# W2 in four loads, nine long throwaway matmuls, the first two tiles normed in three parts, and another written-out order, in a one-core kernel of LayerNorm, a spectral filter and an MLP

## The chip, the cores and the metric

The kernel runs on one core of one Trainium2 chip. The metric is the device time of one execution in microseconds, the lower the better. The core has five engines that work side by side, each through its own list of instructions in the order given: PE (TensorE, matrix products), DVE (VectorE), ACT (ScalarE), POOL (GpSimd) and SP (SyncE, which here only issues transfers). PE reads SBUF, the on-chip memory of 128 partitions, and writes PSUM, 8 banks of 2 KB per partition; DVE and ACT bring results from PSUM back to SBUF. Engines wait for each other through semaphores; a transfer (DMA) has a semaphore of its own.

## What is computed

The input x has 2048 tokens of 640 numbers in bf16. Cut to what matters:

```python
xn = layernorm(x, axis=-1)                       # 2048 x 640
X  = rfft2(xn.astype(float32), axes=(-2, -1))    # over tokens and over the 640
A  = irfft2(X * (w_r + 1j * w_i), s=(2048, 640), axes=(-2, -1)).astype(bfloat16)
h  = gelu(xn @ w1 + b1)                          # 2048 x 1536, tanh form
B  = h @ w2 + b2                                 # 2048 x 640
return x + A + B
```

The weights w1 are 640 x 1536, w2 1536 x 640, and w_r and w_i 2048 x 321.

## The kernel before

**Tiles and stages.** The tokens are cut into 16 tiles c of 128; partition p of tile c holds token 16p + c. All stages of all tiles are unrolled into about 1,100 small steps, each with a name and an engine.

- *Norm.* `x{c}` loads a tile or two (`load_x`, L455). On DVE `st{c}.0` and `st{c}.1` take the statistics of its two halves and `ag{c}` joins them. For the first two tiles `sq` (square root on ACT) and `rs` (reciprocal on DVE) give the inverse deviation, for the others `ve` on DVE and a power `rs` on POOL. `nm{c}` (DVE, L554) writes the normed tile xn. For tile 0 it has two parts, `nm0` (columns 0 to 383) and `nm0.3` (384 to 639); tile 1 has one.
- *Transposes of xn.* For tiles 0 to 3 PE transposes blocks of 128 columns against the identity (`tp`, L568) and ACT or DVE copies the result from PSUM to xnT (`tc`): in two parts for tile 0, in one for the others. Tiles 4 to 15 are transposed by DMA (`td{c}`, L560), issued on SP.
- *MLP, first product* (`h`, through the helper L411). BLOCKS makes seven groups of tiles: 0, 1, (2, 3), (4, 5), (6, 7), (8 to 11), (12 to 15). For tiles 0 and 1, `h{t}.{q}.{j}` are three matmuls of 128 columns: quarter q of the 1536 outputs, block j of the 640 inputs. From h2 on, `h{b}.{f}.0` has three matmuls and `h{b}.{f}.3` two, of 256 columns (h2 to h4) or 512 (h5, h6). `ge` on ACT is the gelu with the bias column b1col, which comes from PE step `b1mm` and ACT copy `b1cp`. A table load on ACT (`table1`, L530) stands ahead of the gelus.
- *MLP, second product.* `k{c}.{o}.{f}` and `l{c}.{o}.{f}` are three matmuls each over gT and W2, in column cuts o (CUTS: 0 to 383, 384 to 639). Ten tiles (KEEP) run early as `k`, and DVE adds x to them at once (`kk`); the others run late as `l` into the same bank as the last step of the spectral branch.
- *Spectral branch.* Folding sums on DVE (`f1`, `f2`), a product along tokens (`G{c}`, copies `gx`), one along the 640 (`b{g}`, copies `xb`), one of 32 x 32 blocks (`c{P}.{r}`, 32 small matmuls, copies `y`), the filter on DVE (`m`, `z`), the way back (`d{P}.{v}`, 32 small matmuls, copies `u`), a transpose by DMA (`vt0` to `vt15`, L706), the way back along the 640 (`e{g}`, copies `yo`), unfolding sums (`y2`, `yf`), and the last product `fin`, one matmul per piece. GROUPS gives b and e steps of three or two tiles. Each `e` step reads all 16 `vt` results. For the groups in NEAR a copy `xr{g}` (DVE or ACT) first brings a part of them next to each other.
- *End.* `os{c}.{o}` (DVE, L811) adds x or the kept sum to fin's bank, and `out` (SP, L818) stores. Tile 15 goes in three pieces (PIECES): 320, 160 and 160 columns, each with its own store; all other tiles have one store.

**Order.** Nothing chooses at run time. The string ORDER lists every step as engine:name; each engine runs its steps in that order, and SLOTS gives each buffer its place (PSUM banks among them). `Plan.place` works out from it what each step must wait for, `Plan.sync` drops waits that others imply, `Plan.emit` writes the programs. So an engine's later step waits behind its earlier one, and on SP every load, transpose and store waits behind the one before it.

**Loads.** All go through SP in ORDER's order, except b1 (ACT). The first ones are x0, x1, half of W1 by rows (`w1_00` to `w1_02`), x2 (which is tiles 2 and 3), `w1_03`, `w1_04`, the other half `w1_10` to `w1_14`. W2 comes in two halves of 960 KB, `w2_0` (of the 12 blocks of 1536 inputs the first six) and `w2_1`.

**Throwaway work.** `idle` (L444) puts matmuls of zeros into a bank that nothing reads: `idle0` 38 at the start and `idle1` 4 between the transposes of tile 0 and of tile 1.

```python
WARM = (38, 4)
...
            pe(name, lambda: [(psb(b.slot, [[1, 128]]), warm, warm, True, True) for _ in range(n)], reads=[B_warm], writes=[b], **kw)
```

Of the kernel before, what the change touches and what calls it, by code (L numbers as in the profile page):

```python
# [851 lines left out]
```

## Time and profile before

| what | value |
|---|---|
| three runs | 147.81, 148.09, 149.21 us (median 148.09) |
| the profiled execution's own time | 147.38 us |
| its span, first to last instruction | 146.1 us |
| busy: PE, DVE, ACT, POOL | 142.4, 116.6, 79.7, 7.3 us |
| DMA packets | 29226, 18.40 MB, mean 126 GB/s |
| HBM read and written | 10.92 MB, 2.62 MB |

The profile is of one execution. Times in it count from the span's start. A row of the timeline reads: start, duration (both us), engine, line, operation, what is written and read, shape, xcount; several instructions in a row are merged into one row, whose duration runs from the first start to the last end. In brackets stands how long the engine sat idle before and what ended that. PEld is the loading of weights into PE, which overlaps PE. SPq rows are the issuing of transfers on SP. A matmul's row starts when it starts reading and ends later than the next one's start, because matmuls are pipelined; so the pace is read from starts, not from durations. Most PE steps share the helper's line L411 and are told apart by what they read: `W,gT` is k or l, `xnT,W` is h, `getab` is e, `T,ntab` is d, `Wf,htab` is fin, `EB` alone is throwaway work. In the table of groups the two numbers behind the count are busy us and the mean ns of one, then the idle time ahead of them.

### The profile page before, as it was taken

What the parts mean: (1) busy time and instruction counts of PE and PEld (TensorE: products, weight loads), DVE (VectorE), ACT (ScalarE), POOL (GpSimd) and SP (SyncE); (2) the same over time, 40 slices, a digit from 0 to 9 for tenths busy, and PEclk for the clock granted to TensorE, in tenths of its full rate; (3) what the DMA queues carried; (4) which work ended last, traced back from release to release, by engine and by line L of the source; (5) the groups of instructions that cost most, each with busy time, mean ns of one, the idle gap of its engine ahead of it and who ended that gap; (6) DMA issues with size and microseconds to landing.
All of it is one profiled execution on the core that took longest, in us unless ns stands there. A gap on an engine that the chain in (4) does not pass through costs nothing.

```text
span 146.1 us, 4167 instructions
## 1 busy us (share of the span) xinstructions
PE 142.4 (97%) x1760; PEld 99.9 (68%) x1760; DVE 116.6 (80%) x272; ACT 79.7 (55%) x149; POOL 7.3 (5%) x24
## 2 busy tenths in 40 slices
PE   7999999999999999999999999999999999999993
PEld 7899889896659776546464443456678677767782
DVE  2999898999899486679899978840279979496993
ACT  3389997998747651578674787881043734100000
POOL 2031103102100000000000000000000000000000
PEclk9999999999999999999999999999999999999999
DMA  4999588698999999000000568267500022021334
GB/s 129 312 384 404 141 194 257 124 74 228 282 234 174 173 178 259 11 4 0 4 2 4 114 120 129 50 131 79 109 0 0 4 85 97 4 77 57 135 134 140
DMA packets 29226, 18.40 MB, mean 126 GB/s; under 512 B 20248, under 2 KB 27928, under 8 KB 29080
## 3 DMA queue, kind: packets, MB, share of 16 engines
q1 hardware_dynamic: 29184, 18.14, 52.5%
q8 instruction: 14, 0.23, 0.7%
q14 instruction: 4, 0.03, 0.1%
q10 hardware_dynamic: 24, 0.00, 0.0%
HBM read 10.92 MB, written 2.62 MB: 93 GB/s over the span
## 4 chain that ended last, share of the span: by engine, by line
PE 95%; DVE 2%; DMA 2%; issue 0%
PE ps L411 93%; DMA X<-in_A_x_dram 2%; DVE U L522 1%; PE ps L568 1%; DVE W L811 0%; DVE T L554 0%; DVE mv L524 0%; DVE rstd L528 0%
## 5 line engine op out<-in xcount | busy, mean ns | idle before, releaser
L411 PE MATMUL ps<-W,gT 128*128 128x256 bf16 (+3 forms) x396 | 58.8, 296 | 0.0
L411 PE MATMUL ps<-xnT,W 128*128 128x256 bf16 (+2 forms) x420 | 57.8, 288 | 0.0
L411 PEld LDWEIGHTS ps<-W,gT 128*128 128x128 bf16 x396 | 36.8, 98 | 15.3 <-issue 1.2
L411 PEld LDWEIGHTS ps<-xnT,W 128*128 128x128 bf16 x420 | 34.4, 98 | 15.2 <-issue 2.4
L640 ACT ACTIVATE gT<-ps,b1col 128x256 bf16<-128x256 f32 (+2 forms) x84 | 36.7, 522 | 8.5 <-PE ps L411 8.4
L421 ACT ACTIVATE Wf<-ps 128x960 bf16<-128x960 f32 (+1 forms) x9 | 7.6, 880 | 17.2 <-PE ps L411 17.2
L522 DVE BATCH_NORM_STATS2 U<-X 128x6 f32<-128x320 bf16 x32 | 14.1, 475 | 2.6 <-DMA X<-in_A_x_dram 2.6
L421 ACT ACTIVATE T<-ps 128x644 bf16<-128x644 f32 (+2 forms) x17 | 9.3, 581 | 8.0 <-PE ps L411 8.0
L421 ACT ACTIVATE XV<-ps 128x1280 bf16<-128x1280 f32 (+1 forms) x8 | 9.5, 1193 | 1.3 <-PE ps L411 1.3
L585 DVE TENSOR_TENSOR T<-T 128x128 bf16<-128x128 bf16 (+1 forms) x32 | 9.0, 311 | 0.1
L811 DVE TENSOR_TENSOR W<-ps,xnT 128x256 bf16<-128x256 f32 (+1 forms) x16 | 7.4, 481 | 1.4 <-DMA out_dram<-W 1.2
L554 DVE TENSOR_SCALAR T<-X,mv,rstd 128x640 bf16<-128x640 bf16 (+2 forms) x17 | 7.0, 433 | 1.6 <-POOL rstd L533 1.3
L422 DVE CAST T<-ps 128x644 bf16<-128x644 f32 x7 | 5.8, 828 | 2.9 <-PE ps L411 2.8
L801 DVE TENSOR_TENSOR xnT<-ps,X 128x384 f32<-128x384 f32 (+1 forms) x16 | 7.7, 484 | 0.6 <-PE ps L411 0.3
L421 ACT ACTIVATE Xb<-ps 128x960 bf16<-128x960 f32 x5 | 6.2, 1262 | 3.4 <-PE ps L411 3.4
L411 PE MATMUL ps<-Wf,htab 128*128 128x256 bf16 (+3 forms) x33 | 8.0, 296 | 0.0
L533 POOL TENSOR_TENSOR rstd<-ve,mhalf 128x2 f32<-128x2 f32 (+1 forms) x8 | 6.1, 768 | 29.1 <-DVE ve L532 29.1
L700 DVE TENSOR_TENSOR T<-T 128x644 bf16<-128x644 bf16 x16 | 7.4, 485 | 0.1
L581 DVE TENSOR_TENSOR T<-T 128x640 bf16<-128x640 bf16 x16 | 7.3, 480 | 0.1
L411 PE MATMUL ps<-EB,XV 32*128 32x160 bf16 (+1 forms) x128 | 7.2, 232 | 0.0
L411 PEld LDWEIGHTS ps<-EB,XV 32*128 32x128 bf16 (+1 forms) x128 | 5.5, 95 | 2.2 <-ACT Xb L421 0.5
L774 DVE TENSOR_TENSOR Wf<-Wf 128x960 bf16<-128x960 bf16 (+1 forms) x12 | 6.8, 595 | 0.1
(62 smaller groups left out, 127.0 us busy)
## 6 DMA issues: line engine op xcount, KB each, us to landing
out_dram<-W SPq DMA_DIRECT2D x15, 160.0 KB, 1.8
X<-in_A_x_dram SPq DMA_DIRECT2D x7, 320.0 KB, 6.6
W<-in_B_w_dram SPq DMA_DIRECT2D x10, 192.0 KB, 4.3
W<-in_B_w_dram SPq DMA_DIRECT2D x2, 960.0 KB, 6.2
Wf<-in_A_w_r_dram SPq DMA_DIRECT2D x7, 160.5 KB, 5.9
Wf<-in_A_w_i_dram SPq DMA_DIRECT2D x7, 160.5 KB, 4.3
gtab<-c_G SPq DMA_DIRECT2D x1, 512.0 KB, 7.4
htab<-c_H SPq DMA_DIRECT2D x1, 512.0 KB, 5.4
```

Source lines behind the costliest of these rows:

```text
L411: ins = e.matmul(o_, lhsT=lw, rhs=rh, start=st, stop=sp_, skip_group_check=True)
L421: return e.activation(dst(), src(), ACT.Copy)
L522: K.op(f"st{c}.{h}", "dve", lambda e, _, c=c, h=h: e.bn_stats(stats[:, c, 6 * h:6 * h + 6], view(X, c * D + H2 * h, [[1, H2]])), reads=[B_ ...
L533: K.op(f"rs{c0}", "pool", lambda e, _, a=a, b=b: e.tensor_tensor(out=rstd[:, a:b], in0=ve[:, a:b], in1=mhalf[:, a:b], op=ALU.pow), reads=[ ...
L554: norm = K.op(f"nm{c}" if not a else f"nm{c}.3", "dve", lambda e, _, c=c, n=n, a=a, b=b, xnv=xnv: e.tensor_scalar(out=xnv(n, a, [[1, b - a ...
L581: K.op(f"f1{pair}.{k}", "dve", lambda e, _, k=k, op=op, xnv=xnv, x1v=x1v: e.tensor_tensor(out=x1v(H2 * k, [[D, 2], [1, H2]]), in0=xnv(0, 0 ...
L585: ring_ops.append(K.op(f"f2{pair}.{k}{i}", "dve", lambda e, _, op=op, x1v=x1v, xfv=xfv, o_=o_, o0=o0, o1=o1, w=w: e.tensor_tensor(out=xfv( ...
L640: K.op(f"ge{bi}.{fc}", "act", lambda e, _, c0=c0, nt=nt, fc=fc, f0=f0, hps=hps: e.activation(gT[:, fc, 128 * c0:128 * (c0 + nt)], psb(hps. ...
L700: return e.tensor_tensor(out=rows, in0=rows, in1=view(TT, TB.slot * 4 * KP + r * KP, [[2 * KP, 2], [1, KP]]), op=op)
L774: K.op(f"yf{gi}.{k}", "dve", lambda e, _, k=k, op=op, y2=y2, yf=yf, n=n: e.tensor_tensor(out=view(Wf, YF + yf.slot * 3 * D + (D - 1) * k, ...
L801: K.op(f"kk{c}.{o0}", "dve", lambda e, _, kps=kps, c=c, home=home, o0=o0, w=w: e.tensor_tensor(out=home[:, o0 // 128:(o0 + w) // 128], in0 ...
L811: K.op(f"os{c}.{o0}", "dve", lambda e, _, c=c, os_=os_, fps=fps, o0=o0, w=w, kept=kept, home=home if kept else None: e.tensor_tensor(out=( ...
```

## The change

- `idle0` becomes nine matmuls of 512 columns (the zeros of `warm` as weights, four times the first 128 columns behind the E table as the other operand); `idle1` goes.
- Tiles 0 and 1 are normed, transposed and copied in three parts (PARTS: block 0, blocks 1 and 2, blocks 3 and 4), each with a PSUM bank; the copies may go to ACT or DVE, and the new order puts all six on ACT. An h step of these tiles waits only for the part that holds its block.
- x2 and x3 are two loads of 160 KB; x3 stands ahead of `w1_10`.
- W2 comes in four quarters of 480 KB, each for three of the 12 blocks, and a k or l step waits for its quarter alone.
- Group 1 joins NEAR: e1 reads a copy `xr1`, made by DVE.
- Tile 15's pieces are 384, 160 and 96 columns.
- ORDER and SLOTS are new throughout; they come from a search that takes in the times of the packets that bring instructions. Of ORDER three stretches stand below: the start, the stretch from d3.0 to e1, and the end.

```diff
+PARTS = (0, 1, 3, 5)
...
-NEAR = (2, 3, 4, 5)
+NEAR = (1, 2, 3, 4, 5)
...
-PIECES = {15: [(0, H2), (H2, Q4), (H2 + Q4, Q4)]}
-WARM = (38, 4)
+PIECES = {15: [(0, 384), (384, 160), (544, 96)]}
+WARM = 9
...
-sp:w1_11 dve:ag1 dve:nm0 act:sq1 pe:b1mm dve:nm0.3 sp:w1_12 pe:tp0.0 dve:rs1 pe:tp0.3 dve:nm1 pe:idle1 sp:w1_13 act:tc0.3 dve:tc0.0 pe:tp1.0 act:b1cp
-sp:w1_14 dve:f10.1 pe:h0.0.0 pe:h0.0.1 act:tc1.0 sp:x4 dve:f10.0 pe:h0.1.0 pe:h0.1.1 sp:x6 pe:h0.0.2 act:table1 pe:h0.1.2 pe:h1.1.0 sp:g pe:h1.1.1
...
-pe:h6.11.3 act:ge6.3 pe:d3.1 pe:h6.0.0 sp:vt9 dve:u7.1 act:u6.1 pe:h6.0.3 act:ge6.11 pe:d3.0 sp:vt8 act:ge6.0 pe:k8.384.0 dve:u7.0 act:u6.0
-pe:k8.384.3 pe:k8.384.6 pe:h6.8.0 sp:vt15 pe:h6.8.3 pe:k11.0.0 act:ge6.8 sp:vt14 pe:k0.0.0 pe:k8.384.9 pe:k0.0.3 sp:vt12 pe:k3.0.0 pe:k3.0.3 pe:k0.0.6
-sp:vt13 pe:k11.0.3 pe:k0.0.9 pe:k11.0.6 dve:kk0.0 pe:k3.0.6 dve:kk8.384 pe:k3.384.0 dve:xr2 pe:k11.0.9 dve:xr5 pe:l6.0.0 pe:k3.384.3 dve:kk11.0
-pe:k3.384.6 pe:k3.384.9 pe:e0 pe:l6.0.3 act:yo0.0 dve:yo0.1 pe:l6.0.6 act:xr4 pe:l6.0.9 dve:kk3.384 pe:e1 dve:y20.0 dve:y20.1 pe:k0.384.0 dve:yf0.1
...
-dve:os14.384 pe:l15.320.6 pe:l15.320.9 dve:os15.0 pe:fin15.320 sp:out14.0 pe:l15.480.0 pe:l15.480.3 dve:os9.384 sp:out15.0 pe:l15.480.6 dve:os15.320
-pe:l15.480.9 sp:out9.0 pe:fin15.480 sp:out15.320 dve:os15.480 sp:out15.480
...
+pool:xbpad1b sp:w1_00 pool:xbpad0a pool:mhalf sp:w1_01 sp:w1_02 dve:st0.0 sp:x2 dve:st0.1 sp:w1_03 dve:st1.0 sp:w1_04 dve:ag0 dve:st1.1 sp:x3 act:sq0
+dve:rs0 sp:w1_10 dve:ag1 dve:nm0.1 act:sq1 dve:nm0 dve:nm0.3 sp:w1_11 pe:tp0.0 dve:rs1 pe:tp0.1 pe:tp0.3 dve:nm1 act:tc0.0 pe:b1mm sp:w1_12 dve:nm1.1
+pe:tp1.0 act:tc0.3 dve:nm1.3 pe:h0.0.0 pe:h0.1.0 act:tc1.0 sp:w1_13 dve:f10.1 pe:tp1.1 act:tc0.1 pe:h1.1.0 dve:f10.0 sp:w1_14 act:tc1.1 pe:h1.0.0
+pe:tp1.3 pe:h0.1.1 dve:st2.0 sp:x4 pe:h1.1.1 act:tc1.3 pe:h1.0.1 dve:st2.1 act:table1 pe:h1.0.2 sp:x6 pe:h1.0.3 pe:h1.1.2 dve:f20.11 dve:ag2 pe:h0.0.1
+sp:g pe:h1.1.3 pe:h0.0.2 dve:st3.0 sp:x8 pe:h1.1.4 pe:h1.0.4 act:b1cp dve:st3.1 pe:h0.3.0 sp:x10 pe:h1.2.0 act:ge1.2 dve:ve2 pe:h0.1.2 dve:ag3
...
+dve:z6.0 pe:h6.5.3 pe:h6.1.0 dve:z6.1 act:ge6.5 pe:d3.1 sp:vt11 act:ge6.8 pe:h6.1.3 dve:u6.1 act:u7.1 pe:h6.0.0 sp:vt9 pe:h6.0.3 pe:d3.0 act:ge6.0
+pe:k8.384.9 sp:vt10 act:u6.0 pe:k11.0.0 dve:kk8.384 pe:k0.0.0 dve:u7.0 act:ge6.1 pe:k11.0.3 sp:vt15 pe:k11.0.6 pe:k0.0.3 pe:k0.0.6 sp:vt13 pe:k0.0.9
+pe:k3.384.0 dve:kk0.0 pe:k11.384.0 sp:vt14 pe:k11.384.3 pe:k3.384.3 pe:k11.0.9 pe:k11.384.6 sp:vt12 dve:kk11.0 pe:k3.0.0 pe:k3.0.3 pe:k3.0.6 pe:k3.0.9
+pe:k3.384.6 dve:kk3.0 pe:k3.384.9 act:xr4 pe:e0 dve:xr5 dve:xr1 pe:k0.384.0 act:yo0.1 dve:yo0.0 pe:k0.384.3 pe:k0.384.6 pe:k0.384.9 pe:l13.0.0
...
+pe:fin10.384 pe:l15.384.0 pe:fin14.0 dve:os10.0 pe:l15.384.3 pe:l15.0.9 dve:os10.384 dve:os14.0 pe:fin15.0 sp:out10.0 pe:l14.384.9 sp:out9.0
+dve:os15.0 pe:fin14.384 pe:l15.384.6 pe:l15.384.9 dve:os14.384 pe:fin15.384 sp:out15.0 dve:os15.384 sp:out14.0 pe:l15.544.0 pe:l15.544.3 pe:l15.544.6
+pe:l15.544.9 pe:fin15.544 sp:out15.384 dve:os15.544 sp:out15.544
...
-            pe(name, lambda: [(psb(b.slot, [[1, 128]]), warm, warm, True, True) for _ in range(n)], reads=[B_warm], writes=[b], **kw)
-        idle("idle0", WARM[0])
+            pe(name, lambda: [(psb(b.slot, [[1, 512]]), warm, view(EB, 800, [[0, 4], [1, 128]]), True, True) for _ in range(n)], reads=[B_warm], writes=[b], **kw)
+        idle("idle0", WARM)
...
-        for h in range(2):
-            load(f"w2_{h}", "sp", W2[:, 6 * h:6 * h + 6, :], w2v[:, 6 * h:6 * h + 6, :], B_w2[h], gate=xlast)
+        for h in range(4):
+            load(f"w2_{h}", "sp", W2[:, 3 * h:3 * h + 3, :], w2v[:, 3 * h:3 * h + 3, :], B_w2[h], gate=xlast)
...
-                parts = ((0, 384), (384, D)) if c == 0 else ((0, D),)
+                parts = [(128 * a, 128 * b) for a, b in zip(PARTS, PARTS[1:])] if c < 2 else [(0, D)]
...
-                    if j0:
-                        idle("idle1", WARM[1], gate=[tp])
...
-                                reads=[B_w1s[h][j], B_xnT[c0][j // 3]], writes=[banks[q]], gate=l1_of[bi][-2:][:1] if j else []))
+                                reads=[B_w1s[h][j], B_xnT[c0][(j + 1) // 2]], writes=[banks[q]], gate=l1_of[bi][-2:][:1] if j else []))
...
-                            reads=[B_w2[f0 // 6]] + [B_gT[c, fc] for fc in range(f0, f0 + 3)], writes=[ps_], gate=K.ops[-1:] if f0 else gate)
+                            reads=[B_w2[f0 // 3]] + [B_gT[c, fc] for fc in range(f0, f0 + 3)], writes=[ps_], gate=K.ops[-1:] if f0 else gate)
```

156 lines of the change are left out of this document (76 added, 80 removed).

## The prediction

> **What bounds the kernel now.** The first view to read is the page's table of engines, then the busy time by stretches, then the chain of work that ended last.
>
> ```profile
> span 146.1 us, 4167 instructions
> PE 142.4 (97%) x1760; PEld 99.9 (68%) x1760; DVE 116.6 (80%) x272; ACT 79.7 (55%) x149; POOL 7.3 (5%) x24
> ...
> 0.00:3.00 3.00, 1.98 (x19) 1.99 (x20) 0.16 (x2) 1.28 (x1) 0.97 (x13) 1.00 0.35 109
> ...
> 143.00:146.10 3.10, 0.54 (x8) 0.33 (x5) 0.69 (x3) 0.00 (x0) 0.00 (x0) 1.00 0.49 162
> ...
> 59.93 83.62 PE ps L411 x1059
> ```
>
> A row of stretches gives each engine's busy time and, in brackets, its instructions; PE stands first. PE is idle for 3.00 - 1.98 = 1.02 us in the first stretch and 3.10 - 0.54 = 2.56 in the last, 3.58 together, and 146.1 - 142.4 = 3.7 us is all its idle time: between 3 and 143 us it rests for 0.1 us. The chain says the same: 83.6 us of it are matmuls in a row. So only three things can move the end: how early PE's real work starts, how much work PE has, and what comes after its last matmul. A new order in the middle can win back only what hides inside "busy", because ends of matmuls are modelled.
>
> How much that is follows from starts of neighbouring matmuls of one size.
>
> ```profile
> 6.78 5.52 PE L411 MATMUL ps<-xnT,W 128*128 128x128 bf16 x96
> 12.14 0.44 PE L568 MATMUL ps<-EB,T 128*128 128x128 bf16 x5
> ...
> 96.54 0.52 PE L411 MATMUL ps<-T,ntab 32*32 32x320 bf16 x32
> 96.99 1.16 PE L411 MATMUL ps<-W,gT 128*128 128x256 bf16 x9
> 97.98 1.24 PE L411 MATMUL ps<-xnT,W 128*128 128x512 bf16 x5
> 99.06 7.65 PE L411 MATMUL ps<-W,gT 128*128 128x384 bf16 x51
> 106.55 0.65 PE L411 MATMUL ps<-getab,XV 128*128 128x160 bf16 x7
> ...
> 118.98 2.12 PE L411 MATMUL ps<-W,gT 128*128 128x384 bf16 x12
> 120.94 0.23 PE L411 MATMUL ps<-getab,XV 128*128 128x160 bf16 x1
> ...
> 142.47 0.99 PE L411 MATMUL ps<-W,gT 128*128 128x160 bf16 x12
> 143.30 0.23 PE L411 MATMUL ps<-Wf,htab 128*128 128x160 bf16 x1
> ```
>
> Per matmul: 5.36/96 = 0.056 us for 128 columns, 0.83/12 = 0.069 for 160, 0.99/9 = 0.110 for 256, 1.96/12 = 0.163 for 384, 1.08/5 = 0.216 for 512; the 32 small ones of a c or d step take 0.45 and cost about 0.1 more where the array changes over to them. Counting all matmuls from 6.78 us at these prices (b and e steps at 1.24 for three tiles, 0.90 for two) gives about 135.9 us; the trace needed 143.37 - 6.78 = 136.6. So at most some 0.65 us of waits are left in the middle.
>
> **The change part by part.** The sum is made against the profiled execution: its own time is 147.38 us, span 146.1 and 1.3 around it. The three other runs have a median of 148.09, so it lies 0.7 below it.
>
> *Start.* These rows carry it.
>
> ```profile
> 1.02 4.35 PE L411 MATMUL ps<-EB 128*128 128x128 bf16 x39 [1.02 <-DVE EB L427]
> 5.02 0.64 DVE L554 TENSOR_SCALAR T<-X,mv,rstd 128x384 bf16<-128x384 bf16 x2
> 5.46 0.72 PE L568 MATMUL ps<-EB,T 128*128 128x128 bf16 x5
> 5.58 0.15 DVE L528 RECIPROCAL rstd<-ve 128x1 f32<-128x1 f32 x1
> 5.76 0.45 DVE L554 TENSOR_SCALAR T<-X,mv,rstd 128x640 bf16<-128x640 bf16 x1
> 5.97 0.63 PE L411 MATMUL ps<-EB 128*128 128x128 bf16 x4
> 6.13 0.35 DVE L422 COPY xnT<-ps 128x384 bf16<-128x384 bf16 x1
> 6.21 0.38 ACT L421 ACTIVATE xnT<-ps 128x256 bf16<-128x256 bf16 x1 [0.79 <-PE ps L568]
> 6.39 0.55 PE L568 MATMUL ps<-EB,T 128*128 128x128 bf16 x5
> 7.70 1.28 ACT L530 ACT_TABLE_LOAD   x1
> ```
>
> The 38 throwaway matmuls and b1mm end near 5.4: 0.107 us each, twice the 0.056 of later ones, though the granted clock stands at 1.00. PE is still at half speed until about 6.6: five transposes and four idle1 take 6.39 - 5.46 = 0.93, the next five only 0.39. Nine of 512 columns at half speed are 9 x 4 x 0.107 = 3.85 us, so idle0 ends at 4.87 instead of 5.07, off the path: the path runs over the norm on DVE.
>
> DVE: nm0's two parts take 0.30 and 0.26 (start to start, from 5.02 to rs1 at 5.58), 640 columns take 0.37; I estimate 0.22 for 128. New: nm0.1 at 5.02, nm0 at 5.28, nm0.3 at 5.50, rs1 at 5.76, nm1 at 5.94, nm1.1 at 6.16, nm1.3 at 6.42. tp0.0 waits for nm0, which is now second: about 5.65, 0.19 later than the 5.46 of before. tp0.1 and tp0.3 follow to 6.18, tp1.0 at 6.31. A copy starts 0.35 after the last transpose's start (5.86 to 6.21) and successive copies on ACT start 0.28 apart. So tc0.0 runs 6.00 to 6.29 and h0.0.0 starts at 6.42; h0.1.0 and tp1.1 end near 6.96; tc1.0 (behind tc0.3 on ACT) ends at 6.99; h1.1.0, h1.0.0 and tp1.3 end at 7.49. Before, the same work (both tiles' transposes and four groups of three) ended at 6.78 + 12 x 0.056 = 7.45. I take **+0.05 us**. Below: idle1 vanishes and nothing replaces it, -0.42 (6.39 - 5.97). Above: one more copy's wait and the first groups at half speed, +0.6. Taking idle1 out gains nothing because the copies of 6.13 and 6.21 are late next.
>
> DVE comes 0.3 later to its next work (6.68 instead of 6.39); tp2.0, which needs nm2 and started at 12.14 without a wait, now comes 23 groups of 0.167 behind 7.49, at 11.3; I estimate a few tenths of cover and cost nothing (if it is short, PE waits by the difference). b1cp moves behind the table load on ACT (about 7.8 to 9.1 with the 1.28 of the row), so b1col is there at 9.3, when the eleventh group behind 7.49 ends that the first gelu needs too: nothing.
>
> *Loads.* x2 and x3 apart: w1_03 and w1_04 have 160 KB less ahead, w1_10 to w1_14 the same bytes and one more issue of 0.47 us on SP.
>
> ```profile
> 4.51 0.43 SPq L406 DMA_DIRECT2D W<-in_B_w_dram  x1
> ...
> W<-in_B_w_dram SPq DMA_DIRECT2D x10, 192.0 KB, 4.3
> W<-in_B_w_dram SPq DMA_DIRECT2D x2, 960.0 KB, 6.2
> ```
>
> w1_10 lands near 4.51 + 4.3 = 8.8; its first user, h0.3.0, comes 11 groups behind 7.49, at 9.3. Cover 0.5 us, nothing on the path; if it is gone, PE waits by what is missing. The quarters of W2 add two issues. Counted on from 7.49 with the prices above, w2_0, half as large, is issued near 19.4 and used by k2.0.0 near 27.8; a landing of 6.2 fits in. w2_2 and w2_3, issued near 33 behind bias2, are first used near 44. Zero.
>
> *Middle.* The matmul counts stay, but for e1: with xr1 its last matmuls read a copy.
>
> ```profile
> L411 PE MATMUL ps<-getab,T 32*128 32x160 bf16 x40 | 1.4, 232 | 0.0
> L411 PE MATMUL ps<-getab,XV 32*128 32x160 bf16 x24 | 0.9, 247 | 0.0
> ```
>
> That is 12 x 15 ns, four at a time: **-0.05**; the copy itself lies on DVE under PE work. The moved transposes (td, vt) and gelus I cost at nothing, with the 0.65 us of waits kept as they are: from -0.65 (all vanish) to +1.1 (the first rival).
>
> *End.* Before:
>
> ```profile
> 143.57 0.32 DVE L811 TENSOR_TENSOR W<-ps,X 128x160 bf16<-128x160 f32 x1 [0.21 <-PE ps L411]
> 143.95 0.43 SPq L818 DMA_DIRECT2D out_dram<-W  x1
> 144.42 0.46 SPq L818 DMA_DIRECT2D out_dram<-W  x1
> L811 DVE TENSOR_TENSOR W<-ps,X 128x384 bf16<-128x384 f32 x5 | 2.7, 548 | 0.0
> L811 DVE TENSOR_TENSOR W<-ps,X 128x256 bf16<-128x256 f32 x5 | 2.1, 415 | 0.4 <-PE ps L411 0.4
> ```
>
> The last add is done at 143.89, but its store is issued at 144.42: SP issues one store each 0.475 us (143.95 to 144.42) and is behind by 0.5. In the new order three stores remain behind out15.0: out14, out15.384, out15.544. Let S be the start of the last matmul, of 96 columns (0.043 each, extrapolated from 0.056 and 0.069). fin15.0 lies 1.60 before S, fin14.384 1.11 before it (0.110 + 7 x 0.069 + 12 x 0.043). An add starts 0.27 after its matmul (143.30 to 143.57). So os15.0 takes DVE from S - 1.33 to S - 0.78 (0.548), os14.384 ends near S - 0.38 (0.415), out14 goes between S - 0.3 and S, out15.384 0.475 later, the last between S + 0.7 and S + 0.95, against S + 1.12 before (144.42 - 143.30). I take **-0.25** (from -0.55, where SP is never late, to +0.2).
>
> Sum: 0.05 - 0.05 - 0.25 = -0.25: 147.1 us against 147.38, and 147.8 against the median. Since I cannot tell on which level the next runs lie, I say 147.5.
>
> **The rivals.** *First, slower: e0 waits for its transposes.* Its matmuls need all 16 vt copies. Before:
>
> ```profile
> 97.15 0.89 DVE L422 CAST U<-ps 128x512 bf16<-128x512 f32 x2 [0.76 <-PE ps L411]
> 98.06 2.42 SPq L706 DMA_TRANSPOSE XV<-U  x1
> 100.52 1.28 SPq L706 DMA_TRANSPOSE XV<-U  x1
> 105.83 0.69 DVE L422 COPY T<-XV 128x256 bf16<-128x256 bf16 x2 [1.45 <-DMA XV<-U]
> ```
>
> d3.0 starts at 96.54, the last copy is there by 105.83, e0 comes at 106.55: 0.7 us to spare. The new order puts fewer matmuls between: 36 of 384 and 24 of 256 columns, 8.5 us, so e0 could start 0.45 + 8.5 = 8.9 us after d3.0 (10.0 before). And DVE does kk8.384 (256 columns) ahead of u7.0: its matmuls end 0.45 + 0.33 after d3.0's start, it follows 0.2 later and holds DVE for 0.35, u7.0 takes 0.89 as in the row, and ends 2.25 us after d3.0's start instead of 98.04 - 96.54 = 1.5. Four transposes of 1.28 + 0.04 and a landing 2.6 after the last issue make 2.3 + 3.95 + 2.6 = 8.85. Nothing is spare. If one takes 2.42 as here, e0 starts 1.1 late: 148.6. It decides from a delay of 0.1. For: the row of 2.42. Against: only one of the last four was so long.
>
> The Trainium skill, Runtime: NRT & Kernel Launch, section Instruction fetch mechanics, says that instructions arrive in blocks of 16 KiB, 256 of them, mostly hidden. The page's queue of 14 instruction packets with 0.23 MB agrees with the size; by it 66 fewer PE instructions move each fetch by a quarter of a block, but no view shows that the 2.42 us was a fetch.
>
> *Second, slower: full speed comes later.* PE idles 0.78 us from 4.87 to 5.65 instead of twice 0.2, and waits more between the transposes. If the way to full speed (1.02 to 6.6, 5.6 us) began again at 5.65, it would end at 11.2: 4.6 us at half speed lose 4.6 x (1 - 0.056/0.107) = 2.2 us: 149.7. For: half speed lasted through 5.5 us of almost gapless work. Against: gaps of 0.2 us did not prevent it.
> The Trainium skill, TensorE: Matmul & The Clock Gate, Part 1, says that a free-running window of about 3.4 us must be busy before full speed is given. By it one window more would cost an estimated 1.6 us; the trace's doubled start distances agree with the two speeds, and no run here shows the windows.
>
> *Third, faster: the waits go.* All 0.65 of the middle and the 0.42 of idle1 vanish: 147.5 - 1.1 = 146.4. For: the sizes are there. Against: the copies of the start, and each wait removed shows the next.
>
> **How the numbers follow.** Forecast 0.61, e0 late 0.18, full speed late 0.07, waits gone 0.14. The range 146.6 to 148.8 leaves out the second rival and most of the third. A measurement here can tell about 1% from no change, 146.6 to 149.6: faster 0.14 (third), slower 0.08 (second, and a little of the first with the second), same 0.78.
>
> **What would show it.** Start: first 128-column matmul on xnT near 6.4, not before tp1.0; the twelfth done near 7.5; distances 0.056 from about 6.6. If 0.107 goes on past 7, the second rival holds. e0: its start less d3.0's, 8.9 if I am right, 10 if late, with a wait for XV in the list. End: last store's issue 0.8 to 0.9 behind the last matmul's start. A PE idle row between 10 and 140, or a DMA row among PE's waits, would make the sum wrong.

## The result, and the profile after

| | before | after |
|---|---|---|
| median of 22 executions each | 148.51 us (147.06 to 149.21) | 149.47 us (148.21 to 151.08) |
| ratio, with its 95% interval | 1 | 1.0076 (1.0055 to 1.0098) |
| the profiled execution | 147.38, span 146.1 | 149.17, span 147.9 |

The forecast was 147.5 us (146.6 to 148.8). The kernel became slower by 0.8%, less than the 1% that the prediction took as the bound for a change in either direction, but its time lies above the range.

The page of the changed kernel begins with:

```profile
span 147.9 us, 4128 instructions
PE 142.7 (97%) x1727; PEld 96.0 (65%) x1727; DVE 119.3 (81%) x273; ACT 80.1 (54%) x155; POOL 7.3 (5%) x24
```

PE is idle for 147.9 - 142.7 = 5.2 us, against 3.7 before. Where, the busy time by stretches tells; PE's busy time stands first behind the length of the stretch. The changed kernel:

```profile
3.00:7.00 4.00, 3.39 (x22) 1.46 (x21) 3.88 (x15) 1.67 (x6) 0.00 (x0) 1.00 0.93 277
7.00:30.00 23.00, 22.46 (x279) 20.43 (x278) 20.56 (x70) 20.44 (x55) 4.58 (x6) 1.00 0.78 241
30.00:60.00 30.00, 29.70 (x279) 21.20 (x278) 25.09 (x61) 17.90 (x29) 1.61 (x2) 1.00 0.92 174
...
100.00:112.00 12.00, 11.59 (x128) 8.20 (x128) 5.18 (x9) 3.79 (x6) 0.00 (x0) 1.00 0.59 85
```

The kernel before, same stretches of the middle:

```profile
7.00:30.00 23.00, 23.00 (x289) 21.01 (x287) 21.59 (x73) 21.19 (x52) 4.65 (x7) 1.00 0.82 246
30.00:60.00 30.00, 30.00 (x327) 21.28 (x327) 24.87 (x57) 18.19 (x30) 1.52 (x2) 1.00 1.03 195
...
100.00:112.00 12.00, 12.00 (x117) 8.84 (x115) 6.04 (x11) 2.74 (x3) 0.00 (x0) 1.00 0.24 44
```

In the middle PE was never idle before; now it rests 0.54, 0.30 and 0.41 us in three places. The timeline of the changed kernel shows what each waits for (start, duration, engine, line; in brackets the idle time before the row and what ended it):

```profile
1.02 4.02 PE L413 MATMUL ps<-EB 128*128 128x512 bf16 x9 [1.02 <-DVE EB L429]
5.62 0.54 PE L569 MATMUL ps<-EB,T 128*128 128x128 bf16 x5 [0.59 <-DVE T L555]
6.40 0.49 PE L413 MATMUL ps<-xnT,W 128*128 128x128 bf16 x6
7.35 0.44 PE L413 MATMUL ps<-xnT,W 128*128 128x128 bf16 x5
...
18.83 0.58 SPq L408 DMA_DIRECT2D X<-in_A_x_dram  x1
22.19 0.49 DVE L523 BATCH_NORM_STATS2 U<-X 128x6 f32<-128x320 bf16 x1 [1.63 <-DMA X<-in_A_x_dram]
23.07 0.34 PE L413 MATMUL ps<-gtab,T 128*128 128x128 bf16 x3 [0.46 <-DVE T L584]
32.92 2.10 SPq L561 DMA_TRANSPOSE xnT<-T  x1
36.45 1.24 PE L413 MATMUL ps<-xnT,W 128*128 128x512 bf16 x5 [0.30 <-issue]
99.97 0.51 PE L413 MATMUL ps<-T,ntab 32*32 32x320 bf16 x32
109.47 1.29 PE L413 MATMUL ps<-getab,XV 128*128 128x160 bf16 x16 [0.41 <-DMA XV<-U]
145.42 0.21 PE L413 MATMUL ps<-Wf,htab 128*128 128x96 bf16 x1
145.83 0.93 SPq L817 DMA_DIRECT2D out_dram<-W  x2
```

- *At 22.4 us, G2 (0.6 us).* The load x14 (tiles 14 and 15) is issued at 18.83 and lands at 22.2, and DVE, whose next step is `st14.1`, does nothing for 1.63 us. Behind it in DVE's list is the fold that G2 multiplies. In the kernel before, x14 landed little earlier, at 21.9, but DVE's list came to `st14.1` only at 26.04, as this row of its timeline shows, so nothing waited:

```profile
26.04 0.49 DVE L522 BATCH_NORM_STATS2 U<-X 128x6 f32<-128x320 bf16 x1
```

- *At 36.0 us, h5.0.0 (0.5 us).* The same delay of DVE makes `td6` to `td9` late, and h5.0.0, which needs td9, starts at 36.45. The delay is not all of it: td9's issue, the row at 32.92, takes 2.10 us where the five ahead of it take 1.22 to 1.28, and a packet that brings instructions starts 0.73 us into it. With an issue of 1.28 and the usual landing 1.4 us behind it, td9 would have been there at an estimated 35.6, before h5.0.0 was due.
- *At 108.9 us, e0 (0.6 us).* The last of the four transposing DMAs lands late, behind one whose issue takes 1.80 us (its chain stands below, at the first rival).
- *At 9.2 us, h0.3.0 (0.24 us).* It waits for `w1_10`. In the list of waits (us in total, times, longest) it is the second row; the first is that of DVE for x, three times, the 1.63 us above among them:

```profile
DVE U L523 <- DMA X<-in_A_x_dram: 4.2, 3, 2.1
PEld ps L413 <- DMA W<-in_B_w_dram: 0.2, 1, 0.2
```

The sum closes. Against the profiled execution of before, tile 1's transposes and the first four groups of three are done at 7.35 instead of 7.45 (-0.1); from there to the last matmul it takes 145.42 - 7.35 = 138.07 instead of 143.30 - 7.45 = 135.85 (+2.2); from the last matmul's start to the end of the span 2.48 instead of 2.80 (-0.3). Together +1.8, and 147.9 - 146.1 = 1.8. The waits of the middle, read from the distance between neighbouring steps less what their matmuls cost, are 0.24 (h0.3.0), 0.63 (G2), 0.46 (h5.0.0), 0.58 (e0) and two of 0.15 and 0.17 at b2 and c1.1: 2.2. The first four make 1.9; the kernel before has two of the size of the others, 0.16 and 0.13, so some 0.3 us of the 2.2 are pinned to no single wait.

### The profile page after: what moved, and what is told of

Same layout as the page of the kernel before. It is cut to its first block, busy times and chain, and to the rows that moved or that the text cites. A ratio compares the mean times of both kernels' runs of the same rounds, so it can differ in the third digit from the quotient of the medians.

```text
span 147.9 us, 4128 instructions
## 1 busy us (share of the span) xinstructions
PE 142.7 (97%) x1727; PEld 96.0 (65%) x1727; DVE 119.3 (81%) x273; ACT 80.1 (54%) x155; POOL 7.3 (5%) x24
## 4 chain that ended last, share of the span: by engine, by line
PE 77%; DMA 8%; SPq 7%; DVE 5%; issue 1%; POOL 0%
PE ps L413 77%; DMA X<-in_A_x_dram 6%; SPq L408 4%; SPq L705 3%; DVE U L523 2%; DMA XV<-U 2%; DVE U L424 1%; SPq L561 1%; DVE T L555 1%; POOL rstd L534 0%; DVE mv L525 0%; DVE T L584 0%; DVE xnT L800 0%; DVE W L810 0%; DVE ve L533 0%
## 5 line engine op out<-in xcount | busy, mean ns | idle before, releaser
L413 PE MATMUL ps<-W,gT 128*128 128x256 bf16 (+3 forms) x396 | 59.6, 296 | 0.0
L413 PE MATMUL ps<-xnT,W 128*128 128x256 bf16 (+2 forms) x420 | 58.6, 288 | 0.4 <-issue 0.3
L423 ACT ACTIVATE Wf<-ps 128x960 bf16<-128x960 f32 (+1 forms) x8 | 6.7, 869 | 11.1 <-PE ps L413 11.1
L423 ACT ACTIVATE T<-ps 128x644 bf16<-128x644 f32 (+2 forms) x18 | 9.9, 588 | 4.4 <-PE ps L413 4.2
L423 ACT ACTIVATE Xb<-ps 128x960 bf16<-128x960 f32 x4 | 5.0, 1260 | 8.1 <-PE ps L413 8.1
L424 DVE CAST T<-ps 128x644 bf16<-128x644 f32 x6 | 5.0, 829 | 3.8 <-PE ps L413 3.8
L413 PE MATMUL ps<-Wf,htab 128*128 128x384 bf16 (+3 forms) x33 | 7.7, 295 | 0.0
L555 DVE TENSOR_SCALAR T<-X,mv,rstd 128x640 bf16<-128x640 bf16 (+2 forms) x20 | 7.5, 405 | 0.1
L424 DVE CAST Xb<-ps 128x960 bf16<-128x960 f32 x4 | 5.0, 1250 | 2.9 <-PE ps L413 2.8
```

The lines of the kernel that those rows point to most:

```text
L413: ins = e.matmul(o_, lhsT=lw, rhs=rh, start=st, stop=sp_, skip_group_check=True)
L423: return e.activation(dst(), src(), ACT.Copy)
L424: return e.tensor_copy(dst(), src())
L555: norm = K.op(f"nm{c}.{a // 128}" if a else f"nm{c}", "dve", lambda e, _, c=c, n=n, a=a, b=b, xnv=xnv: e.tensor_scalar(out=xnv(n, a, [[1, ...
```

## The experiments

Of ORDER the diffs show the steps of one engine alone, around those that move. Every ratio is to the kernel before on the same chip.

**A second look at the kernel before** (b_again, no edit).

> The kernel before once more, for a second profile. If the profile of 147.38 us was a lucky execution (its 22 runs have a median of 148.51), this one shows waits of 0.5 to 1.2 us on PE that the first did not have, and a span of 147 us or more. If the executions differ outside the span or by clock, PE shows the same waits of at most 0.65 us.

Its profiled execution took 148.5 us, near the median, and its timeline isn't that of the one at 147.38:

```profile
1.02 3.81 PE L411 MATMUL ps<-EB 128*128 128x128 bf16 x39 [1.02 <-DVE EB L427]
5.42 0.54 PE L568 MATMUL ps<-EB,T 128*128 128x128 bf16 x5 [0.60 <-DVE T L554]
...
17.58 2.15 SPq L560 DMA_TRANSPOSE xnT<-T  x1
22.02 0.82 PE L411 MATMUL ps<-xnT,W 128*128 128x256 bf16 x6 [0.95 <-ACT gT L640]
```

h3.6.0 starts at 22.02, 1.1 us late. The row names ACT, but td5, which h3.6.0 also needs, lands only at 21.93: its issue takes 2.15 us where the one ahead of it takes 1.31. So the kernel before has a wait of its own that comes and goes; the execution that the prediction took as its measure had none.

**The waits filled one by one.** a_stats_late lets DVE take `st14.1` and `st15.1` later; a_e0_late puts four groups ahead of e0; a_all_three does both and puts three groups ahead of h0.3.0.

```diff
-dve:f21.11 dve:st10.0 dve:ag7 dve:st14.1 dve:f21.10 dve:st9.1 dve:f12.0 dve:st15.1 dve:st11.0
+dve:f21.11 dve:st10.0 dve:ag7 dve:f21.10 dve:st9.1 dve:f12.0 dve:st11.0
...
-dve:f24.01 dve:f24.10 dve:f24.00 dve:st14.0 dve:ag14
+dve:f24.01 dve:f24.10 dve:f24.00 dve:st14.1 dve:st15.1 dve:st14.0 dve:ag14
...
-pe:k3.384.9 pe:e0 pe:k0.384.0 pe:k0.384.3 pe:k0.384.6 pe:k0.384.9 pe:l13.0.0 pe:e1
+pe:k3.384.9 pe:k0.384.0 pe:k0.384.3 pe:k0.384.6 pe:k0.384.9 pe:e0 pe:l13.0.0 pe:e1
...
-pe:h1.0.4 pe:h0.3.0 pe:h1.2.0 pe:h0.1.2 pe:h0.2.0 pe:h0.0.3 pe:h0.0.4 pe:h0.3.1
+pe:h1.0.4 pe:h0.1.2 pe:h0.0.3 pe:h0.0.4 pe:h0.3.0 pe:h1.2.0 pe:h0.2.0 pe:h0.3.1
```

> The changed kernel with st14.1 and st15.1 (statistics of the tiles of the load x14) moved on DVE behind f24.00, to just before st14.0; nothing else. Theory A (the new order asks for transfers before they land): the DVE wait of 1.63 us on X at 20.5 us goes, G2 follows h3.7.3 at once (its 0.63 us of waiting goes), td6 is issued about 1.5 us earlier and h5.0.0 no longer waits for td9 (0.46 plus 0.3 us go). PE's last matmul comes 1.0 to 1.4 us earlier, ratio to the kernel before about 1.000. Theory B (loads and transposes simply move more slowly with the smaller loads and are late whatever the order): another transfer is waited for in its place, h5.0.0 still waits for td9, under 0.4 us is gained. Theory C (the waits of the profile are chance of one execution): no change in time beyond 0.2 us.

> The changed kernel with the four steps k0.384 (12 matmuls of 256 columns, 1.3 us) moved on PE ahead of e0, and kk0.384 on DVE ahead of yo0.0; nothing else. Theory A: the last vt copy lands at 109.4 us after e0's first chance at 108.9, so with 1.3 us more of work ahead e0 waits for nothing, and 0.5 us goes; ratio to the kernel before about 1.004. Rival: what follows e0 (yo0, y2, yf, fin1) is as late as before and PE waits at fin1 or e4 instead: nothing gained, a PE wait between 112 and 116 us.

> The changed kernel with both edits and, on PE, h0.1.2, h0.0.3 and h0.0.4 ahead of h0.3.0, so that w1_10 is first used 0.5 us later. Theory A: the three gains add: 1.0 to 1.4, 0.5 and 0.2 us, together 1.7 to 2.1 us below the changed kernel; ratio to the kernel before 0.993 to 0.998. Theory B: under 0.8 us gained, ratio 1.002 or more. Theory C: no gain, 1.0076 as the changed kernel.

a_stats_late: 148.75 us, ratio 1.0014 (0.9975 to 1.0054). The wait at G2 is gone, but e0 waits more, since all ahead of it comes earlier and one of the four transposing DMAs (the second row) is again long; its timeline:

```profile
101.22 6.50 SPq L705 DMA_TRANSPOSE XV<-U  x4
103.86 2.54 SPq L705 DMA_TRANSPOSE XV<-U  x1
109.21 1.42 PE L413 MATMUL ps<-getab,XV 128*128 128x160 bf16 x24 [1.15 <-DMA XV<-U]
```

a_e0_late (four executions): 150.1 us, 1.0117 (1.0057 to 1.0178). e0's wait falls to 0.16 us, e1 waits 0.85 instead: it needs the banks that e0's copies free, and the four groups that hid that are gone. In this execution PE also ran at half speed for long (below). a_all_three: 148.18 us, 1.000 (0.9963 to 1.0036); G2, h5.0.0, h0.3.0 and e0 wait for nothing, and one wait is left, at e1; its timeline:

```profile
110.25 1.16 DVE L424 CAST Wf<-ps 128x960 bf16<-128x960 f32 x1 [0.54 <-PE ps L413]
111.46 1.05 PE L413 MATMUL ps<-getab,XV 128*128 128x160 bf16 x12 [0.68 <-DVE Wf L424]
```

So the order's four places account for the loss: with them filled, at the price of a new wait of 0.86 us, the changed kernel is as fast as the one before. The expectation of 0.993 to 0.998 is missed by that new wait: the profiled span fell by 1.1 us, from 147.9 to 146.8, and not by 1.7 to 2.1.

**The next wait, three times.** a_four fills e1 with groups from the late product; a_four_warm11 is the same with 11 throwaway matmuls; a_five instead splits the cover between e0 and e1; a_six also fills two waits of 0.43 us that a_five brought.

```diff
-pe:k3.384.9 pe:k0.384.0 pe:k0.384.3 pe:k0.384.6 pe:k0.384.9 pe:e0 pe:l13.0.0 pe:e1
+pe:k3.384.9 pe:k10.0.0 pe:k10.0.3 pe:e0 pe:k0.384.0 pe:k0.384.3 pe:k0.384.6 pe:k0.384.9 pe:l13.0.0 pe:e1
...
-pe:l13.384.3 pe:fin1.0 pe:fin0.0 pe:fin0.384 pe:fin2.384 pe:fin2.0 pe:fin3.384 pe:k10.0.6 pe:k10.0.9
+pe:l13.384.3 pe:k10.0.6 pe:fin1.0 pe:fin0.0 pe:fin0.384 pe:fin2.384 pe:k10.0.9 pe:fin2.0 pe:fin3.384
```

(The first pair is a_five's, against a_all_three; the second a_six's, on top of it. a_five also takes k11.384.9 and its copy earlier. a_four puts l6.0.0, l13.0.3 and l13.0.6 ahead of e1, l6.0.3 to l6.0.9 ahead of e4, and l13.384.0, k11.384.9 and l13.384.3 ahead of e2.)

> The kernel with the three edits (statistics late, k0.384 ahead of e0, w1_10 used later), and l6.0.0, l13.0.3, l13.0.6 moved on PE ahead of e1, l6.0.3, l6.0.6, l6.0.9 ahead of e4, l13.384.0, k11.384.9, l13.384.3 ahead of e2, so that e1 has 1.5 us of other work while e0's copies yo0 free its banks. Theory A: the 0.86 us that PE waited at e1 in the kernel with three edits goes, nothing takes its place; 0.6 to 0.9 us below that kernel, ratio to the kernel before 0.994 to 0.997. Rival: the wait moves on to e4, e2 or fin1, ratio as with three edits, 1.000.

> The same with eleven throwaway matmuls instead of nine: they end near 5.72 us, as tp0.0 is due, so PE does not pause. tp0.0 starts 0.1 us later. Theory D: no execution is left with half speed after 7 us; the median falls by 0.2 to 0.4 us against nine, and the highest times by 1 us. Rival (the moment of full speed is chance and does not depend on a pause of 0.75 us): median as with nine or 0.1 above, the same spread.

> The changed kernel in a_all_three's order, with three moves more around e1: k10.0.0 and k10.0.3 stand ahead of e0 in place of k0.384.0 to .9, which come between e0 and e1; k11.384.9 with its copy kk11.384 comes as soon as k11.384.6 is done. So e0 still has about 1 us of other matmuls ahead of it, and DVE has four groups between e0 and e1 to copy yo0.0 out. Theory (the new order asks for things before they are there, and each place can be filled): the 0.86 us at e1 goes, the profile is near 147.2 and the ratio to the kernel before 0.992 to 0.996. Rival 1: a transposing DMA is again stretched by an instruction packet and e0 waits 0.3 to 1.1 us; ratio 1.000 to 1.004. Rival 2: the wait moves on to fin2.0 or e5, which k10.0.0 and k10.0.3 stood ahead of, 0.3 us or more; ratio 0.996 to 1.000. If part of the executions have TensorE at half speed until 9.5 us, these lie 1.2 to 1.5 us above the others.

> a_five with k10.0.6 ahead of fin1.0 and k10.0.9 ahead of fin2.0, which each waited 0.43 us in a_five for a bank that a copy has to free. Theory: both waits go and none takes their place, the usual time is 147.2 to 147.5 (a_five: 148.1) and the ratio 0.994 to 0.998, with a part of the executions 1.3 us above. Rival: the copies of this stretch are what bounds, and e5 or the last outputs wait as much later: the ratio stays at 1.000 to 1.003.

a_four: 149.96 us, 1.0137 (1.0085 to 1.019): waits of 1.7 us at l13.384.0 and 1.1 at fin1.0, each for a bank. a_four_warm11: 150.13 us, 1.0138 (1.0088 to 1.0189), the same; both are slower than the theory and its rival had it. a_five: 148.4 us, 1.002 (0.9983 to 1.0056); neither e0 nor e1 waits, and fin1.0 and fin2.0 wait 0.43 us each instead. a_six: 148.19 us, 0.9999 (0.9965 to 1.0034); those are gone, and e5 waits 0.96. The timeline of a_six:

```profile
122.37 0.55 DVE L810 TENSOR_TENSOR W<-ps,xnT 128x384 bf16<-128x384 f32 x1
122.97 0.71 PE L413 MATMUL ps<-getab,XV 128*128 128x160 bf16 x7 [0.79 <-DVE W L810]
```

The rival of a_six's expectation holds: as far as these moves tell, the emptying of PSUM banks bounds the stretch from 108 to 123 us, and groups placed in front of one wait are missing at the next.

**The throwaway matmuls.** b_throwaway is the kernel before with nine long ones and no idle1; b_long_idle1 and b_short_no_idle1 make one of these two edits each; a_short and a_six_short take the other way, the 38 short ones and idle1 (right behind tp0.3) in the changed kernel and in a_six; a_five_warm11 is a_five with 11 long ones, which end when the transposes can start.

```diff
-WARM = (38, 4)
+WARM = (9, 4)
...
-        idle("idle0", WARM[0])
+        idle("idle0", WARM[0], 4)
```

(b_long_idle1; the 4 makes each 512 columns long. b_throwaway and b_short_no_idle1 take idle1 out of ORDER and of the code.)

> The kernel before, in its own order, with nine throwaway matmuls of 512 columns and no idle1. Theory A: PE waits for the copies tc0.0 and tc0.3 where idle1 stood; the first h step starts at 6.6 to 6.8 as before, ratio 0.998 to 1.002. Theory D (pauses of PE ahead of the first transposes let half speed last longer in part of the executions): in the profile or in the times a step of about 1 us, ratio 1.003 or more, start distances of 0.107 us on the first h steps.

> The kernel before with nine throwaway matmuls of 512 columns in place of 38 of 128, and idle1 (four of 128 columns after the transposes of tile 0) kept. With b_throwaway (nine long, no idle1: 1.0055) and b_short_no_idle1 it tells which of the two edits makes the half speed of TensorE last until 9.6 us. If it is the end of the throwaway matmuls before tp0.0 (the pause before the transposes): as b_throwaway, 1.003 to 1.009, with part of the executions 1.2 to 1.5 us above the others. If it is idle1 that is missing: 0.998 to 1.002, and the groups of three take 0.16 us each from 6.7 us on in the profile.

> The kernel before with its 38 throwaway matmuls of 128 columns, and without idle1. If the missing idle1 makes the half speed last: 1.003 to 1.009, part of the executions 1.2 to 1.5 us above the others. If it is the pause ahead of tp0.0 alone: 0.998 to 1.002. If neither alone does it, both this kernel and b_long_idle1 are at 0.998 to 1.002.

> The changed kernel with the 38 throwaway matmuls of 128 columns and the four of idle1 (right after tp0.3), as before; its order else unchanged. If the nine long ones cost nothing and the order's waits are the whole loss: as the changed kernel, 149.3 to 149.6, ratio 1.005 to 1.009. If the pause after the nine long ones makes full speed come late in 3 of 22 executions or more: the executions above 150.0 are gone and the ratio falls by 0.001 to 0.003. If the throwaway matmuls are the main loss: 148.5 or less, ratio 1.000 or below. idle1 stands in the way of tile 1's transposes, which would cost 0.1 to 0.4 us at the start.

> a_six with the 38 short throwaway matmuls and idle1 of the kernel before. If the nine long ones without idle1 make full speed come late in part of the executions: a_six has executions 1.2 to 1.5 us above its usual time and this one has none, and its median is level with a_six's or up to 0.4 us above (idle1 stands ahead of tile 1's transposes). If the throwaway matmuls make no difference: the same share of high executions in both.

> a_five with 11 long throwaway matmuls in place of nine, so that they end at about 5.7 us, when the first transposes can start, and TensorE doesn't pause. If the pause makes full speed come late in part of the executions: no execution over 149 us (a_five had 4 of 12 at 149.2 to 149.8), the usual time as a_five's or up to 0.2 us above, ratio 0.996 to 1.000. If the pause has nothing to do with them: the same share above 149 us, ratio 1.000 to 1.004.

| kernel | median us | ratio |
|---|---|---|
| b_throwaway | 149.32 | 1.0055 (1.0015 to 1.0096) |
| b_long_idle1 | 148.0 | 0.9966 (0.9935 to 0.9998) |
| b_short_no_idle1 | 147.55 | 0.9949 (0.9908 to 0.9989) |
| a_short | 151.06 | 1.0161 (1.0113 to 1.0209) |
| a_six_short | 149.55 | 1.0101 (1.007 to 1.0132) |
| a_five_warm11 | 148.19 | 0.9989 (0.9953 to 1.0024) |

In b_throwaway PE stayed at half speed until 9.75 us, and every group of three took 0.32 us instead of 0.17, nine of them, 1.4 us together. Its timeline, whose second row says the same of the transposes:

```profile
1.02 4.14 PE L411 MATMUL ps<-EB 128*128 128x512 bf16 x10 [1.02 <-DVE EB L427]
5.45 1.52 PE L568 MATMUL ps<-EB,T 128*128 128x128 bf16 x10 [0.29 <-DVE T L554]
6.76 3.60 PE L411 MATMUL ps<-xnT,W 128*128 128x128 bf16 x36
```

36 starts in about 3.4 us are 0.095 each on average, against 0.056 at full speed. a_e0_late shows the same till 9.96 us. Neither edit alone had it in its profiled execution, and neither costs time (their ratios lie below every range expected): among these three kernels the loss came only with the pause ahead of the transposes and the missing idle1 together. That both are its cause isn't shown, and they don't always bring it: the changed kernel, a_stats_late, a_all_three, a_four, a_five and a_six have both, and in their profiled executions PE is at full speed by 6.4 us. In the changed kernel's order the verdict turns round: a_six_short is 1.4 us slower than a_six, beside it on the same chip. 0.4 us of it stand at the end, where the issue of one store takes 0.83 us instead of 0.43, and 0.5 at the start, as in a_short, whose first real matmul comes behind idle1 at 6.87 instead of 6.40:

```profile
6.87 0.50 PE L413 MATMUL ps<-xnT,W 128*128 128x128 bf16 x6
...
23.60 0.49 DVE L523 BATCH_NORM_STATS2 U<-X 128x6 f32<-128x320 bf16 x1 [3.01 <-DMA X<-in_A_x_dram]
```

(The second row is x14 again: here DVE waits 3.01 us for it, and G2 1.5. None of a_short's three expectations holds.) a_five_warm11 had no execution above 149 us, where a_five had four of twelve at 149.2 to 149.8, a_six and a_all_three two of twelve each. That is what the pause would do; but the kernel before, with its short matmuls, had nine of 22 above 149 us beside a_five_warm11, so it isn't settled that the pause is the cause.

**The loads** (b_loads: before's order, x2 and x3 apart, W2 in quarters).

```diff
-sp:w1_04 sp:w1_10
+sp:w1_04 sp:x3 sp:w1_10
...
-                first(load_x(2, 2))
...
+                    first(load_x(2 + h, 1))
...
-            load(f"w2_{h}", "sp", W2[:, 6 * h:6 * h + 6, :], w2v[:, 6 * h:6 * h + 6, :], B_w2[h], gate=xlast)
+            load(f"w2_{h}", "sp", W2[:, 3 * h:3 * h + 3, :], w2v[:, 3 * h:3 * h + 3, :], B_w2[h], gate=xlast)
```

> The kernel before, in its own order, with the changed loads alone: x2 and x3 as two loads (x3 ahead of w1_10) and W2 in four quarters (w2_1 behind w2_0, w2_3 behind w2_2). Theory A (the order is the cost): within 0.3 us of the kernel before, ratio 0.997 to 1.003. Theory B (the smaller loads make transfers late in any order): W1 or td copies land 0.3 to 0.6 us later, PE waits for w1_10 or td5, ratio 1.004 or more.

149.56 us, 1.0087 (1.0048 to 1.0125). The order of before takes the statistics of tile 3 ahead of tile 2's, and x3 now comes later; its timeline shows tp2.0 waiting for the norm, and 1.3 us at h3.6.0 for a transposing DMA, td5:

```profile
12.86 0.45 PE L567 MATMUL ps<-EB,T 128*128 128x128 bf16 x5 [0.78 <-DVE T L553]
23.33 0.81 PE L411 MATMUL ps<-xnT,W 128*128 128x256 bf16 x6 [1.29 <-DMA xnT<-T]
```

The new order takes tile 2 first and has no wait at tp2.0. The wait at h3.6.0 is the one that b_again has without the split: td5's issue takes 2.38 us, with an instruction packet 0.72 us into it. So the ratio is the one that theory B expects, but what the profile shows for the split is neither w1_10 nor slower transfers: it is a norm that the old order asks for before x3 is there. The split alone costs in the old order; this part and the order can't be priced apart.

**The end** (b_pieces: before's order with the parts 384, 160, 96; b_pieces_no_idle1 and b_long_pieces add a front from above).

```diff
-PIECES = {15: [(0, H2), (H2, Q4), (H2 + Q4, Q4)]}
+PIECES = {15: [(0, 384), (384, 160), (544, 96)]}
```

> The kernel before with tile 15's column parts of 384, 160 and 96 in place of 320, 160 and 160, all else as before. Theory (the term of the prediction for the end, -0.25 us): from the last matmul to the end of the span 2.4 to 2.5 us in place of 2.73, since the last store issue ends 0.7 to 0.95 us after the last matmul in place of 1.12; the ratio 0.997 to 0.9995. Rival: the order of before has SP's stores in a row there as well, the last store issue doesn't come earlier: tail 2.7 us and ratio 1.000.

> The kernel before with tile 15's parts of 384, 160 and 96, and without idle1; its 38 short throwaway matmuls, its loads and its order stay. b_pieces gave 0.9981 and b_short_no_idle1 0.9949, each within 0.004. If both are gains that add up: 0.992 to 0.996, usual time 147.0 to 147.4. If b_short_no_idle1's gain was a draw of ten executions: 0.997 to 1.000.

> The kernel before with nine long throwaway matmuls, idle1 kept, and tile 15's parts of 384, 160 and 96; loads and order of before. b_long_idle1 gave 0.9966 and b_pieces 0.9981, each within 0.0036. If both are gains that add up: 0.993 to 0.997. If they are draws of ten executions, as b_pieces_no_idle1's sum turned out to be: 0.998 to 1.001.

b_pieces: 148.17 us, 0.9981 (0.9946 to 1.0017); b_pieces_no_idle1: 148.15 us, 0.9991 (0.9955 to 1.0027), so b_short_no_idle1's gain didn't come again; b_long_pieces: 147.93 us, 0.9954 (0.9918 to 0.999), the lowest ratio of these three. But the theory for the parts falls: in b_long_pieces the end comes 2.87 us behind the last matmul's start (146.3 - 143.43), no sooner than before, and in b_pieces later still, since a row of stores ran long (the first of the four took 1.29 us, with an instruction packet that started 0.8 us ahead of it; in b_long_pieces, with none, 0.34):

```profile
143.33 2.76 SPq L818 DMA_DIRECT2D out_dram<-W  x4
143.42 0.21 PE L411 MATMUL ps<-Wf,htab 128*128 128x96 bf16 x1
```

SP needs until 146.09, 2.67 behind the last matmul. When the last matmul starts, three stores are left behind the one under way in the old order, two in the changed kernel, so the 0.3 us that this one gains at its end don't come from the sizes alone. The order of the end alone wasn't tried. b_pieces_no_idle1's profiled execution shows one more wait of the old order, 1.1 us for a half of W2:

```profile
28.79 1.14 PE L411 MATMUL ps<-W,gT 128*128 128x384 bf16 x6 [1.14 <-DMA W<-in_B_w_dram]
```

What b_long_pieces and b_long_idle1 gain may come from td5. They have 58 PE instructions less (29 matmuls and their 29 weight loads), and the packets that bring instructions come at other times. td5 in b_long_pieces' timeline:

```profile
17.39 1.26 SPq L560 DMA_TRANSPOSE xnT<-T  x1
```

And b_again's view of the DMA queues for the 0.1 us from 18.3 (packets, MB, share of the engines):

```profile
q8 instruction: 1, 0.02, 58.6%
```

In b_again an instruction packet falls 0.7 to 0.8 us into td5's issue, and the issue takes 2.15 us; in b_pieces_no_idle1 it does too, and takes 2.18. In the execution of 147.38 the packet started at 18.93, when td5's issue had ended at 18.06. b_long_pieces has none near, its td5 takes 1.26, and PE is busy without a gap from 7 to 30 us. That this is the whole gain of 0.4% is argued from single executions, not shown.

## Why the prediction was wrong, point by point

- **The level.** The sum was made against an execution of 147.38 us and the forecast set at 147.5 "since I cannot tell on which level the next runs lie". The median of before is 148.51, and with the forecast change of -0.25 that makes 148.26: the level alone put the forecast 0.8 us too low. The other 1.2 of the 1.97 us between 147.5 and 149.47 are the change, +0.96 instead of -0.25. The text's own other reading, 147.8 against the three runs' median, was nearer. b_again shows what was missing in the execution: a wait of 1.1 us at td5.
- **Middle, the step that failed:** "The moved transposes (td, vt) and gelus I cost at nothing." They cost 2.2 us against that execution. I had costed the end, the start and e0's chain by their due times, and not the other steps that the new order asks for earlier: `st14.1` on DVE against x14's landing, td9 behind it, h0.3.0 against w1_10. a_all_three shows that these and e0 are the loss. At two of the four places, td9 and e0, an instruction packet stretched an issue by 0.8 and 0.5 us; the old order took issues of 2.60 (td11) and 2.42 (vt15) at the same two places without a wait, the new one has no cover for them.
- **Loads, zero.** "Cover 0.5 us" for w1_10 was short by 0.24, by a slip of the sum: the sentence ahead of it had counted x3's issue of 0.47 us on SP, and "4.51 + 4.3 = 8.8" left it out. With it the landing is 9.3, at the moment when h0.3.0 was forecast; it landed at 9.4, and h0.3.0 was reached at 9.2. W2's quarters cost nothing, as said.
- **Start, +0.05.** Measured -0.1 against the profiled execution; the path was as described (first 128-column matmul on xnT at 6.40 for 6.42, tp0.0 at 5.62 for 5.65). But the five transposes at 5.62 ran at full speed, which I had put at 6.6.
- **End, -0.25.** Measured -0.3; the two last stores are issued from 145.83 to 146.76, so the last one begins 0.9 behind the last matmul's start, as forecast.
- **e1 and xr1, -0.05.** Too small to be read.
- **First rival, e0 late (chance 0.18).** The mechanism was right and the price half: 9.5 us from d3.0 to e0, where 8.9 and 10 had been the two readings. The chain of the changed kernel:

```profile
102.20 1.20 SPq L705
103.40 0.04 issue
103.45 1.28 SPq L705
104.76 1.80 SPq L705
106.61 2.82 DMA XV<-U
```

One issue is longer by 0.5, and the landing takes 2.82 for 2.6. The prediction left open whether its row of 2.42 was a fetch of instructions. The trace of the kernel before has a packet at 98.73, 0.67 us into that issue; its view of the DMA queues for the 0.1 us from 98.7:

```profile
q8 instruction: 1, 0.02, 82.1%
```

The changed kernel has one at 105.19, 0.43 us into the issue of 1.80. The copy u7.0 ended 2.2 after d3.0, as worked out. "Nothing is spare" should have made it the likeliest case, not a rival.
- **Second rival, full speed late (0.07).** It isn't in the changed kernel's profiled execution, and is in those of b_throwaway and a_e0_late, to 9.75 and 9.96 us instead of 11.2, at 1.3 to 1.4 us instead of 2.2. The Trainium skill, TensorE: Matmul & The Clock Gate, Part 1, speaks of a free-running window of about 3.4 us that must be busy. By it an estimated 1.6 us were at stake, nearer than mine. The ends seen are 3.75 (b_pieces_no_idle1), 4.05 (b_again), 6.6 (before) and 9.75 and 9.96, so the moment differs between executions; but 3.75 is only 2.7 us after PE's first matmul at 1.02, which doesn't fit a window that must be busy throughout, and no run shows the windows themselves.
- **Third rival, waits go (0.14).** The opposite came. Its reason against, that each wait removed shows the next, is what a_five and a_six did.

## What to carry to other kernels

When an order is rewritten, list every step that now comes earlier and hold it against the landing of what it reads, on each engine; a step of another engine that stands at the head of its list with nothing to do (DVE at 20.56) delays PE as surely as PE's own wait. Take the level of a forecast from the median of many executions, and look at a second profile before calling the first one's waits all there are. A wait that goes when groups are put ahead of it says little until the next ones are looked at: here 0.86 us went from e1 to fin1.0 and fin2.0 and on to e5.

## What the runs showed of the hardware that was not expected

- *An instruction packet stretches the issue of a transposing DMA.* Counted over the twenty profiles, leaving out 41 to 49 us: of 359 issues with no packet of 16 KB near, 355 took 1.20 to 1.35 us. All 28 with one in their first 0.7 us took longer, 1.39 to 2.77, among them 1.80 (the changed kernel) and 2.54 (a_stats_late). With one 0.7 to 0.85 us in it went either way, 2.15 (b_again) and 2.18 (b_pieces_no_idle1) among the long ones. Later ones left the issue alone, 1.26 and 1.27 with a packet 1.1 and 1.0 us in (b_short_no_idle1, b_pieces), but there the transfer landed 2.6 and 2.2 us behind its issue instead of 1.4 (b_long_pieces). From 41 to 49 us issues ran up to 2.71 us with no packet near, so packets aren't the only cause, and how they act isn't shown. The Trainium skill, Runtime: NRT & Kernel Launch, Instruction fetch mechanics, calls the cost of such fetches mostly hidden; PE's program agrees, since PE rests only 0.1 us between 3 and 143 us in the kernel before, SP's issues don't.
- *PE's full speed comes at a time of its own.* With the same front the 38 short matmuls end their half speed at 4.05 us in b_again (39 in 3.81 us) and not by their end in the execution of 147.38 (39 in 4.35), where it goes on to 6.6. The granted clock reads 1.00 in all of them.
